# Attention and two gated layers on one core: SP's transfers of groups 1 to 7 in program order, stores an iteration behind their data, a third place for words

## The chip, the cores and the metric

The kernel runs on one core of a Trainium2 chip. What counts is the device time of one execution in microseconds. TensorE (PE) multiplies, VectorE (DVE), ScalarE (ACT) and GpSimd (POOL) work on tiles, and SyncE (SP) issues nearly all transfers (DMA).

## The reference

Three stages, all in fp32, over 4608 tokens (8 batches of 576) of 512 features:

```python
q_s = softmax(q, axis=-1)          # over the 64 features of a head, 8 heads
k_s = softmax(k, axis=2)           # over the 576 tokens
kv = einsum('bhsd,bhse->bhde', k_s, v)
x = einsum('bhsd,bhde->bhse', q_s, kv)      # then (tokens, 512)
xn = x / sqrt(mean(x * x) + 1e-6) * rms_g
x2 = (silu(xn @ w_gate) * (xn @ w_val)) @ w_out        # 512 -> 1536 -> 512
h = maximum(maximum(x2 @ w1, x2 @ w2), x2 @ w3)        # 512 -> 768
out = h @ w_out2                                       # 768 -> 512
```

## The kernel before

**Tiling.** The tokens are cut into nine groups g of 512: the first 512 of each batch, and the eight rests of 64 as group 8. An fp32 product is made of three products of split operands (high x high, low x high, high x low, the parts in fp32r). For each group the first layer runs in 12 iterations f, one for each 128 of the 1536 features: `pg`, the gate's product (12 matmuls of 128x512, `product_in`, L558 to L560), `pv`, the value's product (12 more), then t = tanh on ACT (L889), t on DVE (L890), h on DVE (L899), and h's store to DRAM by SP (L900).

**Attention in between.** Within the iterations of a group the next groups' attention is made, head pair p after head pair. For each (g, p) there are loads of kT, q, k, v and qT (q by feature); the maximum of k (`km`, L399), its broadcast through PE (`pb`, L406), the subtraction (L407), the exponential (ACT, L408) and kv (`pk`, L417); the maximum and the reciprocal sum of q, which go to DRAM (`put_stat`) and come back broadcast over the partitions (`spread_stats`, L335, four DMAs), q's softmax on POOL and ACT (`q_softmax`, L348 to L350), and x (`make_x`). When all four pairs are there, the sum of squares (`sacc`, L476) goes through PE (L509), three Newton steps on DVE give 1/rms (`z`, L517), which is stored and read back broadcast (`zb`, L524); `normalise` multiplies x by it (L540), `split_x` makes the high and low parts of x (L99, L100) that the next group's products read. For groups 0, 1 and 2, z is spread by transposes on PE instead (`spread_rstd`, L531). `turn_of` says at which pair of iterations a pair's `make_kv` is due.

**Weights ahead.** The output weights of the first layer and all of the second layer's arrive as 64-bit words. From group 1 on the class `Ahead` (`advance`, once an iteration) loads words (`st`, L216), joins them to fp32 (L225, L226), makes sums of their quarters (L238 to L241), splits seven quarters for each unit (ACT L249, POOL L250) and stores them in DRAM (L251). After group 8 the rest of the kernel, products with seven quarters of each matrix in place of eight, reads h and these quarters back and fills TensorE.

**What sets the order.** The kernel is written as one sequential program. The Tile framework's scheduler lists each engine's instructions by priority and its own estimates of time; `tc.issue_after(ins)` adds an edge that orders an instruction behind another. SP takes its list in order, so a DMA that waits (for a tile, or for a store that it reads) holds all behind it. Buffers are tiles with a tag; a tile waits for the readers of the one that had its place before.

## Time and the profile before

| | us |
|---|---|
| median of 3 runs | 1550.04 |
| lowest, highest | 1545.99, 1551.12 |
| the profiled execution | 1553.54 |
| its span | 1551.4 |
| TensorE busy in it | 1494.7 (96%) |
| VectorE, ScalarE, GpSimd busy | 1057.0, 608.0, 447.4 |

The mean granted clock of TensorE is 0.987. The profiled execution stands 3.5 us above the median of the runs, so what is read in the trace belongs to a time of 1553.54. Busy shares are averages over stages: the iterations of groups 1 to 8 and the part after group 8 are read apart.

### The profile page before, as it was taken

The page shows a single profiled execution, that of the slowest core. Times are in us where ns is not written, and L with a number is a line of the kernel's source. Part 1 is how long each engine was busy: PE and PEld are TensorE (multiplying, and loading weights), DVE is VectorE, ACT ScalarE, POOL GpSimd, SP SyncE. Part 2 cuts the span into 40 slices and gives each one's busy share as a digit, 9 for nine tenths or more (in the row PEclk, how much of TensorE's full clock was granted, in tenths as well). Part 3 has the DMA queues.
Part 4 walks back from the last instruction along what each step waited for, and adds up shares of the span by engine and source line. Part 5 has one row for each costly group of instructions (what it writes and reads, how often), then busy time and mean ns, then how long its engine had stood idle before and what let it go on. Part 6 is the DMA issues. An engine that isn't in the chain of part 4 may idle for free.

```text
span 1551.4 us, 19834 instructions
## 1 busy us (share of the span) xinstructions
PE 1494.7 (96%) x6692; PEld 1229.2 (79%) x6692; DVE 1057.0 (68%) x1777; ACT 608.0 (39%) x1197; POOL 447.4 (29%) x379
## 2 busy tenths in 40 slices
PE   5899999899999999999999999999999999999999
PEld 4677778787878788887877888888888888888887
DVE  6997575666675766364679889927938938837722
ACT  7764333333434343342445445512413413413311
POOL 0012424242524343434347657201111111101100
PEclk9999999999999999999999999999999999999999
DMA  8866777767776766677773453346486486485573
GB/s 274 293 208 183 221 205 239 213 214 221 225 219 214 219 211 198 211 260 278 281 236 130 149 193 116 126 162 238 149 309 225 159 312 223 156 310 189 174 267 108
DMA packets 159333, 330.30 MB, mean 213 GB/s; under 512 B 31104, under 2 KB 55680, under 8 KB 159232
## 3 DMA queue, kind: packets, MB, share of 16 engines
q1 hardware_dynamic: 155776, 322.74, 63.7%
q10 hardware_dynamic: 3456, 6.29, 1.1%
q8 instruction: 53, 0.87, 0.2%
q14 instruction: 48, 0.39, 0.1%
HBM read 246.42 MB, written 82.55 MB: 212 GB/s over the span
## 4 chain that ended last, share of the span: by engine, by line
PE 46%; DVE 5%; DMA 2%; issue 2%; POOL 1%; ACT 0%; SPq 0%; DVEq 0%; ACTq 0%; POOLq 0%
PE p_a L566 4%; PE p_a L565 4%; PE p_a L564 4%; PE o_acc L565 3%; PE o_acc L566 3%; PE o_acc L564 3%; PE p_G L564 2%; PE p_G L566 2%; PE p_G L565 2%; PE o_a L564 2%; PE o_a L566 2%; PE o_a L565 2%; DMA w_dram<-wq 1%; PE p_V L566 1%; PE p_V L565 1%
## 5 line engine op out<-in xcount | busy, mean ns | idle before, releaser
L988 POOL TENSOR_TENSOR temps_wl<-temps_wl,temps_wh 128x512 f32<-128x512 f32 x36 | 48.2, 1339 | 348.5 <-ACT temps_wh L987 273.8
L250 POOL TENSOR_TENSOR wq<-st,wq 128x256 fp32r<-128x256 f32 x126 | 104.0, 841 | 126.9 <-ACT wq L249 111.1
L890 DVE SCALAR_TENSOR_TENSOR t<-t,pg 128x512 f32<-128x512 f32 x106 | 72.5, 684 | 75.6 <-ACT t L889 74.9
L899 DVE SCALAR_TENSOR_TENSOR h<-t,pv 128x512 f32<-128x512 f32 x108 | 73.6, 681 | 29.6 <-PE pv L560 25.4
L249 ACT CAST wq<-st 128x256 fp32r<-128x256 f32 x126 | 51.4, 423 | 93.3 <-DMA w_dram<-wq 49.6
L385 POOL TENSOR_TENSOR q<-q,qm 128x512 f32<-128x512 f32 x28 | 31.4, 1123 | 186.9 <-PE pk L417 95.0
L348 POOL TENSOR_TENSOR qT<-qT,stat 128x512 f32<-128x512 f32 x28 | 38.8, 1386 | 144.0 <-DMA stat<-stats 43.9
L979 DVE TENSOR_TENSOR temps_wl<-temps_wl,p_a 128x512 f32<-128x512 f32 x72 | 49.2, 683 | 37.3 <-POOL temps_wl L988 37.1
L889 ACT ACTIVATE t<-pg 128x512 f32<-128x512 f32 x106 | 62.5, 590 | 24.8 <-PE pg L560 22.2
L225 DVE TENSOR_SCALAR st<-st 128x512 int32<-128x512 int32 x36 | 19.3, 537 | 68.5 <-DMA st<-in_w_out 42.4
L417 PE MATMUL pk<-v,k 128*128 128x129 f32 x300 | 43.5, 294 | 21.6 <-ACT k L408 18.5
L983 ACT COPY temps_wh<-p_G 128x512 f32<-128x512 f32 x36 | 21.1, 587 | 105.7 <-PE p_G L566 105.5
L564 PE MATMUL p_a<-x_wh,chunk 128*128 128x512 f32 x160 | 62.2, 389 | 0.0
L565 PE MATMUL p_a<-x_wh,chunk 128*128 128x512 f32 x160 | 62.2, 389 | 0.0
L566 PE MATMUL p_a<-x_wh,chunk 128*128 128x512 f32 x160 | 62.2, 389 | 0.0
L564 PE MATMUL p_a<-x_wl,chunk 128*128 128x512 f32 x160 | 62.2, 389 | 0.0
L565 PE MATMUL p_a<-x_wl,chunk 128*128 128x512 f32 x160 | 62.2, 389 | 0.0
L566 PE MATMUL p_a<-x_wl,chunk 128*128 128x512 f32 x160 | 62.2, 389 | 0.0
L417 PEld LDWEIGHTS pk<-v,k 128*128 128x128 f32 x300 | 40.0, 204 | 28.0 <-ACT k L408 23.4
L349 ACT ACTIVATE qT<-qT 128x512 f32<-128x512 f32 x28 | 17.7, 632 | 101.5 <-POOL qT L348 101.5
L985 DVE TENSOR_TENSOR temps_wl<-temps_wh,p_V 128x512 f32<-128x512 f32 x36 | 24.6, 684 | 43.9 <-PE p_V L566 43.9
L715 POOL TENSOR_TENSOR h_X<-h_Y,h_X 128x512 f32<-128x512 f32 x24 | 42.6, 1783 | 28.7 <-DVE o_xl L100 15.9
(1202 smaller groups left out, 4885.1 us busy)
## 6 DMA issues: line engine op xcount, KB each, us to landing
chunk<-w_dram SPq DMA_DIRECT2D x112, 768.0 KB, 4.4
w_dram<-wq SPq DMA_DIRECT2D x126, 256.0 KB, 3.5
h_dram<-h SPq DMA_DIRECT2D x108, 256.0 KB, 3.4
stat<-stats SPq DMA_DIRECT2D x112, 128.0 KB, 3.3
words<-in_w SPq DMA_DIRECT2D x24, 512.0 KB, 6.7
chunk<-w_dram SPq DMA_DIRECT2D x48, 256.0 KB, 3.7
k<-in_k SPq DMA_DIRECT2D x30, 320.0 KB, 4.3
v<-in_v SPq DMA_DIRECT2D x30, 320.0 KB, 4.9
```

The lines of the kernel that those rows point to most:

```text
L249: nc.scalar.copy(t[:, 0, :], src)
L250: nc.gpsimd.tensor_sub(t[:, 1, :], src, t[:, 0, :].bitcast(F32))
L417: nc.tensor.matmul(pk[:, 0 : P + 1], k_t[g, p][:, c, :], v_t[g, p][:, c, :], start=(c == 0), stop=(c == 4))
L564: nc.tensor.matmul(pt, ah, bh, start=first, stop=False, skip_group_check=onto)
L565: nc.tensor.matmul(pt, ah, bl, start=False, stop=False, skip_group_check=onto)
L566: nc.tensor.matmul(pt, al, bh, start=False, stop=last, skip_group_check=onto)
L715: nc.gpsimd.tensor_sub(x, y, x)
L889: nc.scalar.activation(t, pg, AF.Tanh, scale=0.5)
L890: nc.vector.scalar_tensor_tensor(t, t, 1.0, pg, op0=ALU.add, op1=ALU.mult)
L899: lows.append(nc.vector.scalar_tensor_tensor(h, t, 0.5, pv, op0=ALU.mult, op1=ALU.mult))
L979: nc.vector.tensor_add(y, x, pt)
L988: nc.gpsimd.tensor_add(w, u2, s5)
```

## The change

Five things are changed. (1) `sp` issues SP's DMAs; from group 1 to the start of group 8 each is ordered behind the one before it in the program. (2) Stores of h, kv, quarters and 1/rms go into a list `later`, which the head of the next iteration issues. (3) Three tiles (`rooms`, in the tags o5, o6, o7) are made once: their plane 0 holds zb, t of odd iterations and qT of odd pairs, the other planes hold four places for split quarters and a third place for words. `advance` loads words at its start, into a place that was released at least one call before. (4) The loads of a pair are in two halves (kT at an even iteration, k and v at the odd one); the statistics of q go to DRAM at the next iteration's start and are read back one iteration later; q's softmax and product come an iteration later; zb is read at the head of iteration at + 2, where `at` is 7 (9 for group 2). (5) In group 8 the load of h's last quarter (W) moves from f = 0 to f = 11.

```diff
+
+        if queue["kept"] and queue["last"] is not None:
+            with tc.issue_after(queue["last"]):
+                ins = nc.sync.dma_start(dst, src).ins
+        else:
+            ins = nc.sync.dma_start(dst, src).ins
+        queue["last"] = ins
+
+    later, rooms = [], {}
+
     class Weights:
 
 
...
+        def release(self, i):
+            if self.held[i] is None or not self.last:
+                self.free.append((self.held[i], self.now + 1))
 
         def load(self):
             i = self.loaded
-            if i < len(self.sources):
-                t = two.tile([P, 2 * N], I32, tag="st", name=f"st2_{i}")
-                nc.sync.dma_start(t, self.sources[i].bitcast(I32))
+            if i < len(self.sources) and self.free and self.free[0][1] <= self.now:
+                t = self.free.pop(0)[0]
+                self.held.append(t)
+                if t is None:
+                    t = two.tile([P, 2 * N], I32, tag="st", name=f"st2_{i}")
+                sp(t, self.sources[i].bitcast(I32))
                 words = t.rearrange("p (n t) -> p n t", t=2)
                 self.st.append((words[:, :, 0], words[:, :, 1]))
...
+            elif self.spots:
+                t = self.spots.pop(0)
+                self.spots.append(t)
+                t = t.rearrange("p (i n) -> p i n", i=2).bitcast(F32R)
             else:
                 t = two.tile([P, 2, N // 2], F32R, tag="y", name=name, bufs=3)
             nc.scalar.copy(t[:, 0, :], src)
             nc.gpsimd.tensor_sub(t[:, 1, :], src, t[:, 0, :].bitcast(F32))
-            nc.sync.dma_start(dst, t.bitcast(F32))
+            if self.spots:
+                later.append((dst, t.bitcast(F32)))
+            else:
+                sp(dst, t.bitcast(F32))
...
+            self.last = last
+            self.load()
             self.apart = f is None
...
+    def load_first(g, p):
         if g < NB:
             kT_t[g, p] = pair_tile(one, [P, 576], F32, "kT", g, p)
-            nc.sync.dma_start(kT_t[g, p], kt[g, p])
+            sp(kT_t[g, p], kt[g, p])
...
+
+    def load_second(g, p):
         if g < NB:
             k_t[g, p] = pair_tile(two, [P, 5, P], F32, "k", g, p)
-            nc.sync.dma_start(k_t[g, p], k[g, p])
+            sp(k_t[g, p], k[g, p])
...
+        qT[g, p] = rooms["qT"] if p % 2 else two.tile([P, N], F32, tag="qT", name=f"qT_{g}_{p}", bufs=1)
+        sp(qT[g, p], qt[g - BY_FEATURE, p])
...
-        put_stat(g, p, 1, qr)
+        qrec[g, p] = qr
...
-        put_stat(g, p, 0, qm)
+        qmax[g, p] = qm
...
-        nc.sync.dma_start(kv_dram[p, :, g, :], raw)
+        if g == 0:
+            sp(kv_dram[p, :, g, :], raw)
+        else:
+            later.append((kv_dram[p, :, g, :], raw))
...
-            nc.sync.dma_start(rstd_dram[g].rearrange("(r t) -> r t", t=4), z)
-            zb = wpool.tile([P, N], F32, tag="o5", name=f"zb_{g}")
-            nc.sync.dma_start(zb, rstd_dram[g].unsqueeze(0).to_broadcast([P, N]))
-            rstd[g] = None, zb
+            later.append((rstd_dram[g].rearrange("(r t) -> r t", t=4), z))
+
+    def read_rstd(g):
+        sp(rooms["zb"], rstd_dram[g].unsqueeze(0).to_broadcast([P, N]))
+        rstd[g] = None, rooms["zb"]
...
+        if g == 1 and f == 0:
+            queue["kept"] = True
+            planes = [wpool.tile([P, 3, N], F32, tag=tag, name=f"rooms_{tag}") for tag in ("o5", "o6", "o7")]
+            rooms.update({name: x[:, 0, :] for name, x in zip(("zb", "t", "qT"), planes)})
+            second.spots = [x[:, i, :] for i in (1, 2) for x in planes[0:2]]
+            second.free.append((planes[2][:, 1:3, :].rearrange("p i n -> p (i n)").bitcast(I32), 0))
+        if nxt is None and f == 0:
+            queue["kept"] = False
+            second.spots = []
+        for dst, src in later:
+            sp(dst, src)
+        later.clear()
...
@@ -838,30 +890,37 @@
             for t in due(-1):
                 make_x(*t)
             for t in due(0):
-                q_by_feature(*t)
+                q_softmax(*t)
                 make_kv(*t)
+            for t in due(1):
+                put_stat(*t, 1, qrec[t])
+                load_by_feature(*t)
+            if due(2):
+                for t in due(2):
+                    load_first(*t)
+                with tc.issue_after(lows[-1].ins):
+                    for t in due(2):
+                        first_stats(*t)
+        else:
             for t in due(2):
-                load_pair(*t)
+                put_stat(*t, 0, qmax[t])
+                load_second(*t)
             for t in due(1):
-                load_by_feature(*t)
                 spread[t] = spread_stats(*t)
             if due(2):
                 with tc.issue_after(lows[-1].ins):
                     for t in due(2):
-                        first_stats(*t)
-        else:
-            if due(2):
-                with tc.issue_after(lows[-1].ins):
-                    for t in due(2):
                         k_max(*t)
-            for t in due(2):
-                q_stats(*t)
+                        q_stats(*t)
             for t in due(1):
                 k_exp(*t)
-                q_softmax(*t)
+            for t in due(0):
+                q_by_feature(*t)
         if nxt is not None and nxt >= BY_FEATURE:
             if f == at:
                 token_rstd(nxt)
+            if f == at + 2 and nxt not in COMPACT:
+                read_rstd(nxt)
             if f == 10:
...
-            t = wpool.tile([P, N], F32, tag="o6", name=f"t_{g}_{f}")
...
-        nc.sync.dma_start(h_dram[g][f // 3][:, f % 3, :], h)
+        later.append((h_dram[g][f // 3][:, f % 3, :], h))
...
                 second.load()
+                second.load()
             second.advance(f, nxt is None)
         if nxt is None:
...
-                for name in "XZYW":
+                for name in "XZY":
                     load_h(0, name)
+            if f == NF1 - 1:
+                load_h(0, "W")
...
+    for dst, src in later:
+        sp(dst, src)
```

DVE in group 2 before, round iteration 8, where group 3's x (xraw_3_p) is multiplied by zb_3 and the maximum is taken from k of group 4's pair 0 (k_4_0):

```order
L540 TENSOR_TENSOR xraw_3_0_2255<-xraw_3_0_2255,zb_3_2720 128x512
L890 SCALAR_TENSOR_TENSOR t_2_8_2789<-t_2_8_2789,pg_2_8_2776 128x512
L341 TENSOR_SCALAR qs_4_1_2818<-qs_4_1_2818 128x8
L540 TENSOR_TENSOR xraw_3_1_2399<-xraw_3_1_2399,zb_3_2720 128x512
L343 RECIPROCAL qr_4_1_2821<-qs_4_1_2818 128x8
L540 TENSOR_TENSOR xraw_3_2_2518<-xraw_3_2_2518,zb_3_2720 128x512
L899 SCALAR_TENSOR_TENSOR h_2_8_2805<-t_2_8_2789,pv_2_8_2792 128x512
L399 TENSOR_REDUCE km_4_1_2816<-kT_4_1_2757 128x1
L407 TENSOR_TENSOR k_4_0_2647<-k_4_0_2647,pb_4_0_2824 128x640
```

The same place now; the line of dots leaves out the nine rows up to t_2_10:

```order
L949 SCALAR_TENSOR_TENSOR t_2_8_2744<-t_2_8_2744,pg_2_8_2731 128x512
L958 SCALAR_TENSOR_TENSOR h_2_8_2760<-t_2_8_2744,pv_2_8_2747 128x512
L435 TENSOR_REDUCE km_4_1_2779<-kT_4_1_2723 128x1
L376 TENSOR_REDUCE qs_4_1_2781<-q_4_1_2613 128x8
L443 TENSOR_TENSOR k_4_0_2656<-k_4_0_2656,pb_4_0_2786 128x640
...
L949 SCALAR_TENSOR_TENSOR t_2_10_2877<-t_2_10_2877,pg_2_10_2864 128x512
L580 TENSOR_TENSOR xraw_3_0_2233<-xraw_3_0_2233,rooms_o5_1432 128x512
L580 TENSOR_TENSOR xraw_3_1_2373<-xraw_3_1_2373,rooms_o5_1432 128x512
L580 TENSOR_TENSOR xraw_3_2_2490<-xraw_3_2_2490,rooms_o5_1432 128x512
L580 TENSOR_TENSOR xraw_3_3_2606<-xraw_3_3_2606,rooms_o5_1432 128x512
L958 SCALAR_TENSOR_TENSOR h_2_10_2893<-t_2_10_2877,pv_2_10_2880 128x512
```

k_4_0's subtraction has moved ahead of group 3's four products with zb, which now stand two iterations later, behind t_2_10.

SP in group 2 before, round iterations 10 and 11, with the broadcast (stat_4_2) of the statistics of group 4's pair 2, the words st2_9 and k's load:

```order
L328 DMA stats_4_2_173<-qr_4_2_2958 128x2x4
L251 DMA w1_dram_7_149<-wq_3_2_3095 128x512
L335 DMA stat_4_2_3047<-stats_4_2_173 64x512
L900 DMA h_dram_2_3_117<-h_2_10_2950 128x512
L292 DMA kT_4_3_3040<-in_kt 128x576
L335 DMA stat_4_2_3047<-stats_4_2_173 64x512 x3
L251 DMA w1_dram_10_152<-wq_3_1_3099 128x512
L216 DMA st2_9_3103<-in_w1_out 128x1024
L900 DMA h_dram_2_3_117<-h_2_11_3008 128x512
L297 DMA k_4_3_3042<-in_k 128x640
```

SP in group 2 now, round iterations 9 and 10 (rooms_o5 in the second row is zb, in the later ones places of split quarters; rooms_o7 is qT):

```order
L142 DMA stat_4_0_2774<-stats_4_0_171 64x512 x4
L142 DMA rooms_o5_1432<-rstd_3_194 128x512
L142 DMA h_dram_2_3_117<-h_2_9_2819 128x512
L142 DMA w1_dram_4_146<-rooms_o5_1432 128x512
L142 DMA w1_dram_16_158<-rooms_o6_1433 128x512
L142 DMA w1_dram_13_155<-rooms_o5_1432 128x512
L142 DMA stats_4_1_172<-qr_4_1_2784 128x2x4
L142 DMA rooms_o7_1434<-in_qt 128x512
L142 DMA kT_4_2_2852<-in_kt 128x576
L142 DMA q_4_3_2854<-in_q 128x512
L142 DMA st2_9_2895<-in_w1_out 128x1024
L142 DMA kv_dram_200<-kv_raw0_213 128x128
L142 DMA h_dram_2_3_117<-h_2_10_2893 128x512
```

The broadcasts stand together, behind the loads of k and v and ahead of the zb read; h_2_9's store follows at the head of iteration 10, with the statistics, and the words st2_9 stand with the loads.

POOL in group 1 before, near the end, with the last sum of squares of group 2 (sacc_2) and q of group 3:

```order
L476 TENSOR_TENSOR sacc_2_1569<-sacc_2_1569,sq_2_2_1843 128x512
L348 TENSOR_TENSOR qT_3_0_1971<-qT_3_0_1971,stat_3_0_1973 128x512
L350 TENSOR_TENSOR qT_3_0_1971<-qT_3_0_1971,stat_3_0_1973 128x512
L385 TENSOR_TENSOR q_3_1_1872<-q_3_1_1872,qm_3_1_1980 128x512
L476 TENSOR_TENSOR sacc_2_1569<-sacc_2_1569,sq_2_3_1963 128x512
```

POOL at the same place now:

```order
L421 TENSOR_TENSOR q_3_1_1854<-q_3_1_1854,qm_3_1_1963 128x512
L515 TENSOR_TENSOR sacc_2_1567<-sacc_2_1567,sq_2_3_1953 128x512
L275 TENSOR_TENSOR rooms_o6_1433<-st2_3_1812,rooms_o6_1433 128x256
L421 TENSOR_TENSOR q_3_2_1961<-q_3_2_1961,qm_3_2_2116 128x512
L384 TENSOR_TENSOR qT_3_0_1957<-qT_3_0_1957,stat_3_0_2010 128x512
L386 TENSOR_TENSOR qT_3_0_1957<-qT_3_0_1957,stat_3_0_2010 128x512
```

qT_3_0's two steps, which read the broadcast statistic, have moved from ahead of the last sum to behind it.

## Rows read from the trace of the kernel before

**Rows 1.** Windows (busy us of PE, PEld, DVE, ACT, POOL; clock, DMA share, GB/s).

```profile
611.60:684.30 72.70, 72.70 (x346) 61.32 (x346) 37.51 (x71) 29.45 (x59) 25.32 (x29) 1.00 0.67 213
756.50:1551.40 794.90, 787.17 (x3457) 647.44 (x3455) 558.59 (x766) 283.07 (x489) 200.01 (x127) 1.00 0.57 197
125.80:756.50 630.70, 605.67 (x2765) 502.78 (x2764) 389.34 (x762) 237.51 (x466) 239.31 (x229) 0.98 0.74 226
```

**Rows 2.** TensorE's waits: us in total, times, longest.

```profile
PE pk L417 <- ACT k L408: 18.5, 12, 4.2
...
PE pv L558 <- DVE h L899: 3.6, 1, 3.6
PE pv L509 <- POOL sacc L476: 3.2, 1, 3.2
PE rstd L531 <- DVE z L517: 2.8, 1, 2.8
```

**Rows 3.** Windows as in group 1, the six at the low clock.

```profile
121.30:124.70 3.40, 3.40 (x10) 2.55 (x10) 3.40 (x7) 3.18 (x6) 0.00 (x0) 0.50 0.63 169
186.20:193.00 6.80, 6.80 (x21) 5.64 (x22) 6.26 (x17) 2.95 (x7) 4.13 (x6) 0.50 0.69 211
278.30:285.10 6.80, 5.09 (x17) 4.50 (x18) 6.80 (x14) 2.47 (x5) 2.14 (x2) 0.50 0.80 241
363.70:367.10 3.40, 3.40 (x10) 2.62 (x9) 3.35 (x10) 0.63 (x1) 1.51 (x1) 0.50 1.00 269
442.20:449.00 6.80, 6.15 (x19) 5.32 (x20) 6.80 (x11) 2.22 (x4) 2.60 (x2) 0.50 0.78 236
711.90:718.60 6.70, 6.02 (x14) 4.82 (x15) 2.00 (x4) 1.80 (x5) 1.74 (x3) 0.50 0.75 237
```

**Rows 4.** Timeline, groups 2 and 5: start, duration, engine, [idle before, releaser].

```profile
268.33 0.32 SPq L524 DMA_DIRECT2D zb<-rstd  x1
...
274.56 0.69 DVE L540 TENSOR_TENSOR xraw<-xraw,zb 128x512 f32<-128x512 f32 x1 [2.28 <-DMA zb<-rstd]
...
278.38 0.81 DVE L407 TENSOR_TENSOR k<-k,pb 128x640 f32<-128x640 f32 x1
...
279.22 0.74 ACT L408 ACTIVATE k<-k 128x640 f32<-128x640 f32 x1 [0.81 <-DVE k L407]
...
280.01 2.52 PE L417 MATMUL pk<-v,k 128*128 128x129 f32 x10 [4.17 <-ACT k L408]
...
522.09 0.38 PE L417 MATMUL pk<-v,k 128*128 128x129 f32 x1 [1.05 <-ACT k L408]
```

**Rows 5.** Timeline, group 3: words, their join, pk.

```profile
295.86 0.43 SPq L216 DMA_DIRECT2D st<-in_w_out  x1
...
302.75 0.43 DVE L225 TENSOR_SCALAR st<-st 128x512 int32<-128x512 int32 x1 [3.31 <-DMA st<-in_w_out]
...
309.17 0.60 PE L417 MATMUL pk<-v,k 128*128 128x129 f32 x3 [0.74 <-ACT k L408]
```

**Rows 6.** SP's waits (total, times, longest), and zb's landing.

```profile
SPq L335 <- DMA stats<-qm: 18.4, 9, 3.6
SPq L335 <- DMA stats<-qr: 18.0, 16, 2.8
...
DMA to landing us min/median/max: 4.6/5.2/7.0
```

**Rows 7.** Timeline, group 1: POOL round the last sum of squares.

```profile
178.90 1.29 POOL L348 TENSOR_TENSOR qT<-qT,stat 128x512 f32<-128x512 f32 x1 [8.73 <-DMA stat<-stats]
...
184.69 1.27 POOL L476 TENSOR_TENSOR sacc<-sacc,sq 128x512 f32<-128x512 f32 x1
```

**Rows 8.** Timeline, group 8: words and their join.

```profile
696.02 0.44 SPq L216 DMA_DIRECT2D st<-in_w_out  x1
...
704.08 1.01 DVE L225 TENSOR_SCALAR st<-st 128x512 int32<-128x512 int32 x1 [3.04 <-DMA st<-in_w_out]
```

**Rows 9.** Timeline, group 0: words in DVE's chain.

```profile
119.81 0.41 DVE L225 TENSOR_SCALAR st<-st 128x512 int32<-128x512 int32 x1
```

More of the change, by code (lines that the diff above doesn't have):

```diff
@@ L134, in attention_moe_moe, with sp @@
     wh, wl = {}, {}
+    queue = {"last": None, "kept": False}
+    def sp(dst, src):
+        if queue["kept"] and queue["last"] is not None:
[5 more added lines that the diff above has]
+    later, rooms = [], {}
     class Weights:
@@ L150, in load @@
                     src = w1[f].rearrange("p j n -> p (j n)")[:, h * HALF : (h + 1) * HALF]
-                    nc.sync.dma_start(t, src.bitcast(I32))
+                    sp(t, src.bitcast(I32))
                     words = t.rearrange("p (n t) -> p n t", t=2)
@@ L204, in __init__ @@
             self.loaded, self.st, self.now, self.apart = 0, [], 0, False
-            self.issued, self.turn = [], False
+            self.issued, self.turn, self.spots = [], False, []
+            self.free, self.held, self.last = [(None, 0), (None, 0)], [], False
             self.steps = []
@@ L208, in __init__ @@
                 self.steps += [(self.join, (2 * u,)), (self.join, (2 * u + 1,)), (self.sums, (u,))]
-                self.steps += [(self.quarter, (u, n)) for n in (A11, A12, S3, S4)] + [(self.load, ())]
-                self.steps += [(self.quarter, (u, n)) for n in (A22, S1, S2)] + [(self.load, ())]
+                self.steps += [(self.quarter, (u, n)) for n in (A11, A12, S3, S4)] + [(self.release, (2 * u,))]
+                self.steps += [(self.quarter, (u, n)) for n in (A22, S1, S2)] + [(self.release, (2 * u + 1,))]
+        def release(self, i):
+            if self.held[i] is None or not self.last:
+                self.free.append((self.held[i], self.now + 1))
         def load(self):
             i = self.loaded
-            if i < len(self.sources):
-                t = two.tile([P, 2 * N], I32, tag="st", name=f"st2_{i}")
-                nc.sync.dma_start(t, self.sources[i].bitcast(I32))
+            if i < len(self.sources) and self.free and self.free[0][1] <= self.now:
[4 more added lines that the diff above has]
+                sp(t, self.sources[i].bitcast(I32))
                 words = t.rearrange("p (n t) -> p n t", t=2)
@@ L271, in advance @@
                 writes = step == self.quarter
-                cost = 0 if step == self.load else 1 if writes else 2
+                cost = 0 if step == self.release else 1 if writes else 2
                 if cost > room or writes and not last and f > 9:
@@ L286, in load_q @@
         q_t[g, p] = pair_tile(two, [P, 8, 64], F32, "q", g, p)
-        nc.sync.dma_start(q_t[g, p], q[g, p])
+        sp(q_t[g, p], q[g, p])
     def load_pair(g, p):
+        load_first(g, p)
+        load_second(g, p)
+    def load_first(g, p):
         if g < NB:
             kT_t[g, p] = pair_tile(one, [P, 576], F32, "kT", g, p)
-            nc.sync.dma_start(kT_t[g, p], kt[g, p])
+            sp(kT_t[g, p], kt[g, p])
         if g < BY_FEATURE:
             load_q(g, p)
+    def load_second(g, p):
         if g < NB:
             k_t[g, p] = pair_tile(two, [P, 5, P], F32, "k", g, p)
-            nc.sync.dma_start(k_t[g, p], k[g, p])
+            sp(k_t[g, p], k[g, p])
             if (g, p, "v") in early or len(v_rooms) < 2:
@@ L308, in load_pair @@
             v_t[g, p] = place
-            nc.sync.dma_start(place[:, :, 0:P], v[g, p])
+            sp(place[:, :, 0:P], v[g, p])
         else:
@@ L313, in load_pair @@
                 t = two.tile([P, 4, P], F32, tag=("k", "v")[i], name=f"kv8_{p}_{i}")
-                nc.sync.dma_start(t, kv_dram[p, :, 4 * i : 4 * i + 4, :])
+                sp(t, kv_dram[p, :, 4 * i : 4 * i + 4, :])
                 kv8[p].append(t)
     qsum = {}
-    qT, spread = {}, {}
+    qT, spread, qmax, qrec = {}, {}, {}, {}
     def load_by_feature(g, p):
-        qT[g, p] = two.tile([P, N], F32, tag="qT", name=f"qT_{g}_{p}", bufs=1)
-        nc.sync.dma_start(qT[g, p], qt[g - BY_FEATURE, p])
+        qT[g, p] = rooms["qT"] if p % 2 else two.tile([P, N], F32, tag="qT", name=f"qT_{g}_{p}", bufs=1)
+        sp(qT[g, p], qt[g - BY_FEATURE, p])
     def put_stat(g, p, i, stat):
         dst = stats_dram[NPAIR * g + p][i].rearrange("a (r t) -> r a t", t=4)
-        nc.sync.dma_start(dst, stat.rearrange("r (a t) -> r a t", a=2))
+        sp(dst, stat.rearrange("r (a t) -> r a t", a=2))
     def spread_stats(g, p):
@@ L534, in spread_rstd @@
         else:
-            zb = wpool.tile([P, N], F32, tag="o5", name=f"zb_{g}")
+            zb = rooms["zb"]
         nc.scalar.copy(zb, pr)
@@ L572, in attention_moe_moe @@
         load_pair(0, p)
-    nc.sync.dma_start(gain, rms_g)
+    sp(gain, rms_g)
     first.load(0)
@@ L671, in out_weights @@
                 t = wpool.tile([P, 2, 2, N // 2], F32R, tag=tag, name=f"w1q_{tag}")
-                nc.sync.dma_start(t.bitcast(F32), w1_dram[len(wq1)])
+                sp(t.bitcast(F32), w1_dram[len(wq1)])
                 wq1.append(t)
@@ L680, in load_h @@
             t = wpool.tile([P, 3, N], F32, tag=tag, name=f"h_{pr}_{name}{j}")
-            nc.sync.dma_start(t, h_dram[g][2 * half + j])
+            sp(t, h_dram[g][2 * half + j])
             for i in range(3):
@@ L881, in iteration @@
         if odd and 0 < g < NB:
-            t = wpool.tile([P, N], F32, tag="o6", name=f"t_{g}_{f}")
+            t = rooms["t"]
         else:
```

2 lines of the change are left out of this document (1 added, 1 removed).

## The prediction

> **What bounds the kernel now.** I read the sums by stage first, then the waits of TensorE, then the stretches at the low clock, and last the timeline round each wait. After group 8 (from 756.50 us) TensorE is busy 787.17 of 794.90 us with 3457 matmuls, 0.2277 us each, at clock 1.00. The eight groups ahead of it, 125.80 to 756.50, where nearly all that the change moves stands, hold 605.67 busy in 630.70 [rows 1]. So TensorE is the bound and only what makes it idle or slow can be won. An iteration's 24 matmuls take 24 x 0.2277 = 5.46 us. Group 7 shows what a group without any such loss looks like: busy for all of its 72.70 us, clock 1.00 [rows 1].
>
> Who makes TensorE wait: ACT's exponential of k (12 waits, 18.5 us), and once each DVE's h (3.6), POOL's sum of squares (3.2) and DVE's z (2.8) [rows 2]. Six stretches at a granted clock of 0.50, the lower of its two levels (1.2 against 2.4 GHz), follow or overlap such waits: TensorE was busy 3.40 + 6.80 + 5.09 + 3.40 + 6.15 + 6.02 = 30.86 us in them, half of which, 15.4, is lost [rows 3]. The waits named in this paragraph that were followed by the low clock are of 2.8 to 4.2 us; that of 1.05 at 522.09 was not [rows 2 to 4]. The waits sum to 18.5 + 3.6 + 3.2 + 2.8 = 28.1; with the clock 43.5 us are at stake.
>
> **A: the wait at iteration 9 of groups 2 to 5.** The read of 1/rms (zb) was issued at 268.33; DVE stood 2.28 us for it and multiplied at 274.56; the subtraction of k's maximum, behind three of these products, came at 278.38, the exponential at 279.22, pk at 280.01 after an idle 4.17. In four groups this idle time is 4.17, 3.50, 2.96 and 1.05 (the first and the last of them are shown) = 11.7; three of the four have a low stretch, busy 5.09 + 3.40 + 6.15 = 14.64, so 7.3 lost [rows 3, 4]. After the change DVE's rows have k_4_0's subtraction four rows behind t_2_8, and the four products eleven and more rows later, behind t_2_10. DVE was idle from 272.28; subtraction 0.81 and exponential 0.74 from there end before 274, and pk was free to start at 280.01 - 4.17 = 275.84. Nearly 2 us are in hand. Removed: 19.0, all of it.
>
> **What A puts in its place.** The products now stand two iterations behind the statistic, near the next group's start. SP's rows have the zb read behind four broadcasts at the head of iteration 9. At 0.32 to 0.43 us an issue [rows 4, 5] it leaves at about 275.4 in the time of before, and it lands 4.6, 5.2 or 7.0 us later (least, median, most) [rows 6]: at 282.4 at the latest, where t_2_10 would be done at about 281.2 (275.84, 1.3 for pk, which is half of the 2.52 that its row shows at the low clock, 2.7 for 12 matmuls, 1.3 for tanh and t). From there DVE has four products at 0.69 [rows 4], three steps of t and h, q's low part and four low parts of x, twelve of 128x512 at 0.69, k_4_1's subtraction (0.81) and two small ones (0.3): 9.4 us, so the last low part is there at 290.6. pk (1.3), two iterations (10.92) and some 2.3 of products and transposes of the attention between them bring TensorE to group 3 at about 290.3, and it wants the low parts one after another until about 292. The chain just fits. Price below: nothing; above: a wait as long as the worst landing brings it, 2.8 idle and 1.7 of clock at each of six group starts. I take 0.7 at each, 4.2, since the estimate leaves about 1 us and the single terms were seen to vary by more.
>
> **B: group 2's sum of squares.** POOL waited 8.73 us for the broadcast statistic and took q of pair 0 ahead of the last sum, which ended at 185.96, when TensorE had been idle 3.2 [rows 2, 7]. In the new rows of POOL the sum stands ahead of that q, behind an instruction of pair 1 that needs no broadcast. Idle 3.2 and half of 6.80 at the low clock, together 6.6, go.
>
> **C: the other waits for k's exponential**, 18.5 - 11.7 = 6.8 us in eight places. One of them: weight words for the joins were issued at 295.86, DVE stood 3.31 for them until 302.75, and pk waited 0.74 at 309.17 [rows 5]. With a third place the words leave an iteration or two earlier; by SP's rows st2_9 stands at about 280 where it is wanted at about 292. Where words were late this goes; where DVE and ACT have other work ahead of k it stays. Bounds 0 and 6.8 left; I leave half, 3.4.
>
> **D: group 8.** The words issued at 696.02 reached DVE at 704.08 (3.04 idle); that instruction took 1.01 where its twin at 302.75 took 0.43 [rows 5, 8]. h_8_3 was late and TensorE idle 3.6, then 6.02 at half speed: 6.6 in all [rows 2, 3]. The change takes the load of h's last quarter out of iteration 0 and so the queue at the words' place is shorter, but POOL and DVE keep their work. Bounds 0 and 6.6; half left, 3.3. The load, now at iteration 11, lands under the products of the part after, where TensorE is full; if that cover were gone it would cost its landing, some 5 us, once.
>
> **E: group 1's rstd.** Work on weight words stood inside DVE's chain (0.41 at 119.81), TensorE idle 2.8, then 3.40 at half speed: 4.5 [rows 2, 3, 9]. These words now stand behind the chain, but the transposes are asked for 10 matmuls (2.3 us) earlier. Bounds 0 and 4.5; I leave 1.0, since the h and the maximum that stood in the chain are behind it too.
>
> **Edits costed at nothing.** The stores that go an iteration later (h, kv, quarters) have their readers two groups or more later. q's softmax and product one iteration later: px that uses them moves with them, and q has the same number of iterations to the next step. The splits' room in other tiles takes away a wait for a buffer and adds none that stands on TensorE's path. If a store's delay held a tile, DVE's h would wait for SP: the cover is the second h tile, which leaves 5.46 us.
>
> SP's own queue is the disputed cost. It has some 80 issues in a group (counted in its order), near 35 of 73 us at 0.44 each [rows 1, 8], so half of its time is free. In the order of before, SP waited for the statistics' own stores ahead of the broadcasts, 18.4 us in 9 places and 18.0 in 16, 2.0 and 1.1 us each [rows 6]. The new order has nine other DMAs, 9 x 0.43 = 3.9 us, between the second statistic's store and its broadcasts, so by these rows the stand is gone. The Trainium skill, "DMA: Bandwidth & Descriptors", section "Two DMAs through the same engine are not ordered", says that placing a store and its read on one queue does not order them: the issuing engine must wait for the store's completion before it issues the read. The trace agrees that SP stands there; by that rule, in an order that nothing may overtake, everything behind the read stands too, and the sum stays as it is only as long as other issues fill the time. Without the page, the same mechanism is the fourth rival below.
>
> **The sum.** 43.5 - 3.4 (C) - 3.3 (D) - 1.0 (E) - 4.2 (new waits) = 31.6. The profiled execution took 1553.54 us (span 1551.4): 1521.9. It stood 3.5 over the median of the runs, 1550.04, so **1519 us** there.
>
> **The rivals.**
> - Forecast, 1519 (own range 1510 to 1528): 0.68.
> - x late at the starts of groups 3 to 8: if zb lands after 282.4 or DVE runs 2 us behind, 2.8 idle and 1.7 clock at six places, 27 in place of 4.2: 1541. For it: the chain just fits. Against: the worst landing seen [rows 6] still fits. 0.12.
> - pk's waits stay, since DVE's and ACT's own queues set them: only B, E and half of D are won, 6.6 + 3.5 + 3.3, less some 1.5: 1538. Against: DVE stood idle 2.28 for a DMA [rows 4]. 0.10.
> - Slower: SP stands in an order that nothing may overtake. A store of h that waits for DVE, or a broadcast that waits for a store, now holds the loads of k, v and the words behind it; before, the schedule let others pass. SP's free half of a pair of iterations is 5 to 6 us; past that, with the two iterations that loads have in hand, from 8 to 10 us a pair of iterations, each us more stands on TensorE in some 24 pairs. At 2 us more: 48 less the gain of 31.6, about 1566. Against: the free half, and the words ahead of need. 0.05.
> - The order moves but the waits only change places: 1550. 0.05.
>
> Changes under 0.3% (4.65 us) can't be told from none here. Faster by more: 0.68 + 0.12 + 0.10 less a little of these tails, 0.87. Within it 0.06, slower 0.07. The range goes from all 43.5 won (1510.0, less 3.5: 1507) to past the two middle rivals (1542).
>
> **What would show it.** Right: no row of pk waiting for ACT over 2 us in groups 2 to 5; POOL's last sum of group 2 ahead of its q; groups 2 to 6 near 73 to 76 us; fewer than three low stretches; DVE not idle for zb. Wrong: TensorE idle at the first product of a group for a low part of x; SP's waits longer for the stores of h; DVE idle for words as before; the part from group 8's end on other than 795 us.

## The result and the profile after

The changed kernel takes 1528.19 us (median of 4 runs, 1525.93 to 1528.61), beside 1548.01 for the kernel before (4 runs, 1543.64 to 1551.12): ratio 0.9871, 95% interval 0.9842 to 0.9900. The profiled execution took 1527.82 us, its span 1526.0, mean clock 0.996. It answers the 1553.54 of before: 25.7 us less, where the medians differ by 19.8, so a size read by comparing the two traces is in part the spread of single executions.

By windows (columns as in [rows 1]), groups 1 to 8 of the changed kernel and the part after group 8:

```profile
125.00:728.07 603.07, 594.25 (x2765) 494.08 (x2764) 387.65 (x764) 240.33 (x466) 234.38 (x225) 1.00 0.79 237
728.07:1526.00 797.93, 788.33 (x3457) 647.13 (x3455) 563.29 (x767) 283.14 (x491) 206.09 (x133) 1.00 0.57 198
```

The groups took 27.6 us less than in [rows 1], the part after them 3.0 more. TensorE's waits in the changed kernel (total, times, longest):

```profile
PE rstd L571 <- DVE z L556: 5.2, 2, 2.7
...
PE px L497 <- DVE ql L100: 4.0, 7, 0.9
...
PE pk L453 <- ACT k L444: 1.3, 2, 0.9
...
PE pv L548 <- POOL sacc L515: 1.0, 1, 1.0
```

Against [rows 2] the wait for k's exponential is down from 18.5 to 1.3, that for the sum of squares from 3.2 to 1.0, that for h in group 8 is gone. New are a second wait for z and seven small ones for q's low part. Of the low clock's six stretches [rows 3] two are left, of 3.41 us each: one answers to the first of before, the other stands behind the new wait for z (columns as in [rows 1]):

```profile
118.04:121.45 3.41, 3.41 (x10) 2.63 (x9) 3.25 (x6) 2.35 (x4) 0.00 (x0) 0.50 0.20 77
193.14:196.55 3.41, 3.41 (x15) 3.21 (x14) 2.95 (x5) 1.75 (x3) 2.71 (x2) 0.50 0.88 319
```

The timeline of group 2 in the changed kernel, as [rows 4]:

```profile
267.36 0.81 DVE L443 TENSOR_TENSOR k<-k,pb 128x640 f32<-128x640 f32 x1
...
270.45 0.41 SPq L142 DMA_DIRECT2D rooms_o<-rstd  x1
...
276.44 2.60 DVE L580 TENSOR_TENSOR xraw<-xraw,rooms_o 128x512 f32<-128x512 f32 x4
```

k's subtraction is 3 us ahead of the read of 1/rms (here rooms_o), and no product of this group waits for that. The group began at 208.7, so the read goes out 61.8 us into it; in the kernel before it went out after 56.8 (268.33 - 211.5). The read has become later, not earlier.

### The profile page after: what moved, and what is told of

It reads as the page before. It is cut to its first block, busy times and chain, and to the rows that moved or that the text cites. A ratio compares the mean times of both kernels' runs of the same rounds, so it can differ in the third digit from the quotient of the medians.

```text
span 1526.0 us, 19735 instructions
## 1 busy us (share of the span) xinstructions
PE 1484.5 (97%) x6692; PEld 1220.3 (80%) x6692; DVE 1060.2 (69%) x1777; ACT 609.0 (40%) x1197; POOL 447.6 (29%) x379
## 5 line engine op out<-in xcount | busy, mean ns | idle before, releaser
L949 DVE SCALAR_TENSOR_TENSOR t<-t,pg 128x512 f32<-128x512 f32 x64 | 43.8, 684 | 62.4 <-ACT t L948 61.8
L275 POOL TENSOR_TENSOR rooms_o<-st,rooms_o 128x256 fp32r<-128x256 f32 x63 | 50.4, 807 | 113.8 <-ACT rooms_o L274 109.2
L958 DVE SCALAR_TENSOR_TENSOR h<-t,pv 128x512 f32<-128x512 f32 x66 | 45.0, 682 | 24.7 <-PE pv L600 22.3
L948 ACT ACTIVATE t<-pg 128x512 f32<-128x512 f32 x64 | 37.8, 590 | 39.4 <-PE pg L600 38.8
L949 DVE SCALAR_TENSOR_TENSOR rooms_o<-rooms_o,pg 128x512 f32<-128x512 f32 x42 | 28.5, 678 | 28.8 <-ACT rooms_o L948 28.8
L757 POOL TENSOR_TENSOR h_Y<-h_W,h_Y 128x512 f32<-128x512 f32 x24 | 39.0, 1639 | 25.3 <-DMA h_W<-h_dram 24.9
L759 POOL TENSOR_TENSOR h_Z<-h_Z,h_X 128x512 f32<-128x512 f32 x24 | 40.0, 1685 | 11.0 <-DVE h_X L752 8.4
L948 ACT ACTIVATE rooms_o<-pg 128x512 f32<-128x512 f32 x42 | 24.8, 590 | 42.5 <-PE pg L600 42.4
```

The costliest lines, as they stand in the source:

```text
L275: nc.gpsimd.tensor_sub(t[:, 1, :], src, t[:, 0, :].bitcast(F32))
L759: nc.gpsimd.tensor_sub(z, z, x)
L948: nc.scalar.activation(t, pg, AF.Tanh, scale=0.5)
L949: nc.vector.scalar_tensor_tensor(t, t, 1.0, pg, op0=ALU.add, op1=ALU.mult)
L958: lows.append(nc.vector.scalar_tensor_tensor(h, t, 0.5, pv, op0=ALU.mult, op1=ALU.mult))
```

## The experiments

All times are medians; ratios are to the kernel before, which ran beside each.

**1. SP's order left to the scheduler.** In the changed kernel one line is left out, so that nothing orders SP's transfers:

```diff
-            queue["kept"] = True
```

> The changed kernel, but the order of SP's transfers in groups 1 to 7 is left to the scheduler, which then puts the first product with zb ahead of h_2_8 and of k_4_0's subtraction again in group 2, and the four products right behind the subtraction in group 3. Theory (DVE's place for these products is what costs, and SP's fixed order is what moves it): pk waits for ACT again in group 2, 2 to 4 us and the low clock behind it, less in groups 3 to 5; in all 5 to 15 us over the changed kernel, 1533 to 1543. Rival (the places, the third words and the later stores bring the gain, SP's order nothing): within 4 us of the changed kernel's 1528.

Measured 1557.88 us, ratio 1.0048 (1.0030 to 1.0066): slower than before, and far over the theory's figure. All the rest of the change without the fixed order is worth less than nothing. In group 2 a product does stand ahead of k's subtraction again and pk waits 2.27 there, as the theory has it, but that is one wait of many. TensorE's waits in this kernel:

```profile
PE pk L453 <- ACT k L444: 16.7, 8, 5.2
PE pv L548 <- POOL sacc L515: 7.1, 4, 2.7
```

and SP's own:

```profile
SPq L144 <- DMA stats<-qm: 35.2, 19, 4.2
SPq L144 <- DMA stats<-qr: 30.7, 15, 3.8
```

SP stands 65.9 us for the statistics' stores. In the kernel before it was 36.4 [rows 6], in the changed kernel 10.1, by its one row:

```profile
SPq L142 <- DMA stats<-qr: 10.1, 5, 2.9
```

In group 2 the scheduler's list has three other transfers between the second statistic's store and its first read, the changed kernel's eight. The store and the read without the fixed order, then with it:

```profile
267.86 0.37 SPq L144 DMA_DIRECT2D stats<-qr  x1
...
270.89 0.45 SPq L144 DMA_DIRECT2D stat<-stats  x1
```

```profile
260.51 0.43 SPq L142 DMA_DIRECT2D stats<-qr  x1
...
267.68 2.55 SPq L142 DMA_DIRECT2D stat<-stats  x4
```

How much of TensorE's loss comes of this stand was not tried by itself.

**2. The products' place alone.** The kernel before with an edge that keeps the four products with zb behind h of iteration 9:

```diff
-            if f == 10:
+            if f == 10 and nxt in COMPACT:
                 for p in range(4):
                     normalise(nxt, p)
+            if f == 10 and nxt not in COMPACT:
+                with tc.issue_after(lows[-1].ins):
+                    for p in range(4):
+                        normalise(nxt, p)
```

(COMPACT are groups 0 to 2, whose z is spread by transposes.)

> The kernel before with one edge more: the four products with zb in groups 2 to 7 are ordered behind the h of iteration 9, so that k's subtraction stands ahead of them; SP's order, stores and places are as before. Theory (the place of the products alone makes the waits at iteration 9): the four waits of 11.7 us and the low clock of 7.3 go, 12 to 19 us off the kernel before, so 1529 to 1536. Rival (SP's late transfers hold DVE there whatever its order): waits of over 2 us at the same place stay, and the time is within 5 us of the kernel before.

Measured 1545.94 us, ratio 0.9976 (0.9960 to 0.9992): 2.8 us off, far from the theory's 12 to 19 and in the rival's time. The rival's waits came only in part: of the four waits at iteration 9 two are gone, the others are 2.10 and 0.54, so 2.6 of 11.7 us is left there. Group 2, where the longer one is:

```profile
266.62 0.44 SPq L524 DMA_DIRECT2D zb<-rstd  x1
...
273.97 0.81 DVE L407 TENSOR_TENSOR k<-k,pb 128x640 f32<-128x640 f32 x1
...
276.67 2.15 PE L417 MATMUL pk<-v,k 128*128 128x129 f32 x10 [2.10 <-ACT k L408]
```

The group began at 210.3, so the read, 56.3 into it, is as late as before (56.8): at iteration 9 the products' place alone does most of the work. But pk waits 15.1 us in all, still 12 times. The timeline at the end of group 3 in this kernel:

```profile
367.73 0.68 DVE L100 TENSOR_TENSOR xl<-xraw,xh 128x512 fp32r<-128x512 f32 x1
...
370.26 0.81 DVE L407 TENSOR_TENSOR k<-k,pb 128x640 f32<-128x640 f32 x1
...
371.10 0.74 ACT L408 ACTIVATE k<-k 128x640 f32<-128x640 f32 x1 [3.57 <-DVE k L407]
...
371.89 1.39 PE L417 MATMUL pk<-v,k 128*128 128x129 f32 x8 [2.49 <-ACT k L408]
```

DVE now makes two of x's low parts just ahead of the next pair's k, and pk waits there, at iteration 11 (2.49, 2.39 and 2.50 at the ends of groups 3, 4 and 5). Most of the wait moved by two iterations.

**3. The order alone.** The kernel before with SP's transfers of groups 1 to 7 chained in its own program order, nothing else:

```diff
-        nc.sync.dma_start(h_dram[g][f // 3][:, f % 3, :], h)
+        sp(h_dram[g][f // 3][:, f % 3, :], h)
...
+        if g == 1 and f == 0:
+            queue["kept"] = True
+        if nxt is None and f == 0:
+            queue["kept"] = False
```

(`sp` is the function of the change; all of SP's transfers of these groups go through it, of which one is shown.)

> The kernel before with SP's transfers of groups 1 to 7 chained in its own program order and nothing else: 1/rms is read back right behind its store, statistics right behind theirs, stores stand where their data are made. Theory (a fixed order pays only when the program is laid out for it): SP stands in it for DVE's chain and for landings, the loads behind come late, and pk, the sums of squares and the words wait more; 5 to 40 us over the kernel before, 1555 to 1590. Rival (program order in itself is what brings the gain): 5 to 20 us under it, 1530 to 1545.

Measured 1534.57 us, ratio 0.9892 (0.9862 to 0.9922). My theory falls, the rival holds: the order alone brings 15 of the 20 us. The theory took the statistics' reads to stand right behind their stores in this order; in the trace seven other transfers lie between (store at 252.53, first read at 264.00), and SP stands 9.7 us for the second statistic's store. Its timeline in group 2:

```profile
258.80 0.32 SPq L142 DMA_DIRECT2D rstd<-z  x1
...
260.88 0.32 SPq L142 DMA_DIRECT2D zb<-rstd  x1
...
265.31 1.29 DVE L551 TENSOR_TENSOR xraw<-xraw,zb 128x512 f32<-128x512 f32 x2 [1.74 <-DMA zb<-rstd]
...
267.78 0.81 DVE L418 TENSOR_TENSOR k<-k,pb 128x640 f32<-128x640 f32 x1
```

DVE takes two of the products ahead of k's subtraction as the scheduler has it, and TensorE does not wait in iteration 9 of any group. The group began at 206.6, so k's subtraction stands 61.2 us into it; in the kernel before 278.38 - 211.5 = 66.9. The read was issued 54.3 into the group against 56.8, and DVE's first product came 4.4 us behind it against 6.2 [rows 4]. Of the 5.7 us 4.3 are the earlier first product, 1.4 the fewer steps of DVE between it and the subtraction.

So with two products still ahead of the subtraction, an earlier read and DVE's shorter way behind it clear iteration 9. The changed kernel clears it the other way: its read is later than before, and the subtraction stands ahead of the products. Neither the products' place nor the late read is the cause by itself: the place alone takes 9.0 of the 11.7 us (experiment 2), the order alone all of it.

The order brings more than this one wait: that for the sum of squares falls from 3.2 to 1.1, that for h in group 8 is gone, and DVE stands 30.9 us for weight words where it stood 64.4. Groups 1 to 8 take 610.7 us (630.7 before), the part after them 799.0 (794.9). How the 15 us split among these was not tried. What is left over the changed kernel is mostly pk's waits at iteration 1 (1.5 to 2.0 in each of groups 2 to 6):

```profile
PE pk L428 <- ACT k L419: 12.1, 8, 2.4
```

**4. Stores at once.** The changed kernel, `later` not used:

```diff
-        later.append((h_dram[g][f // 3][:, f % 3, :], h))
+        sp(h_dram[g][f // 3][:, f % 3, :], h)
```

(and the same for kv, quarters and 1/rms.)

> The changed kernel, SP's fixed order kept, but every store (h, kv, quarters, 1/rms) is issued where its data are made instead of at the head of the next iteration. Theory (in a fixed order a store that waits for its data holds the loads behind it, so the later list is what makes the order bearable): SP stands for DVE's h and POOL's quarters in the middle of an iteration, and loads and broadcasts come later; 4 to 15 us over the changed kernel, 1532 to 1543. Rival (SP has half of its time free, so the place of the stores does not matter): within 2 us of 1528.

Measured 1535.57 us, ratio 0.9910 (0.9889 to 0.9932): inside the theory's range. px waits for q's low part 7.0 us in place of 4.0, o_acc once 4.1. The loss is shown; that it comes of SP's stand for h and the quarters is the theory's reading.

**5. Two places for words.** The changed kernel without the third place:

```diff
-            second.free.append((planes[2][:, 1:3, :].rearrange("p i n -> p (i n)").bitcast(I32), 0))
...
-                second.load()
```

(the last line is the first load into that place.)

> The changed kernel without the third place for words. Theory (the third place brings the words ahead of need, which took away the small waits of pk and the wait for h in group 8): waits for k's exponential come back in part, and more words are left for the part after group 8; 3 to 8 us over the changed kernel, 1531 to 1536. Rival (DVE's order alone took these waits away): within 2 us of 1528.

Measured 1552.10 us, ratio 1.0019 (1.0003 to 1.0034): 24 us lost, three times the theory's upper figure. Little of it lies where the theory put it. The windows of this kernel, and two waits in the part after group 8:

```profile
127.80:734.07 606.27, 595.10 (x2765) 493.93 (x2764) 375.47 (x758) 236.82 (x461) 222.33 (x220) 1.00 0.77 231
734.07:1552.80 818.73, 793.32 (x3456) 650.71 (x3455) 562.65 (x774) 285.90 (x496) 203.78 (x137) 0.99 0.56 196
```

```profile
786.42 0.48 SPq L144 DMA_DIRECT2D st<-in_w_out  x1
...
789.47 0.42 ACT L274 CAST wq<-st 128x256 fp32r<-128x256 f32 x1 [5.27 <-DMA w_dram<-wq]
...
792.68 0.68 ACT L245 ACTIVATE st<-st 128x512 f32<-128x512 f32 x1 [0.71 <-DMA st<-in_w_out]
...
793.24 2.18 ACT L99 CAST o_xh<-h_X 128x512 fp32r<-128x512 f32 x4
...
795.58 0.77 PE L604 MATMUL o_acc<-o_qh,w1q_wl 128*128 128x512 f32 x1 [7.44 <-ACT o_xh L99]
...
823.54 0.42 ACT L274 CAST wq<-st 128x256 fp32r<-128x256 f32 x1 [2.64 <-DMA w_dram<-wq]
...
824.49 0.79 PE L604 MATMUL o_acc<-o_qh,w1q_wh 128*128 128x512 f32 x1 [8.75 <-ACT temps_wh L801]
```

The groups take 3.2 us more than with three places, the part after them 20.8. There 16 quarters are left (13 in the changed kernel), the last 90 us behind group 8's end. Ahead of the work of ACT that the products want stand its steps on quarters and words, and these wait: 5.27 and 2.64 us for an earlier quarter's store, 0.71 for late words. The two waits of TensorE, 7.44 and 8.75, are 16.2 of the 20.8 us.

**6. Two places, refilled at once.** As 5, but a released place is loaded again in the same call:

```diff
-                self.free.append((self.held[i], self.now + 1))
+                self.free.append((self.held[i], self.now))
+                self.load()
```

> The changed kernel with two places for words, each filled again at once when it is released, in place of an iteration later. Theory (the kernel with two places lost 24 us because a place stays empty for an iteration, so that 16 quarters were left after group 8, the last of them 90 us behind its end; the third place pays for that delay): some 10 quarters are left, the last within 50 us of the end, and the part after group 8 is 795 to 799 us; 1528 to 1535. Rival (three words in flight are needed in themselves): 1540 or more, with the waits of 7 and 9 us in the part after group 8.

Measured 1529.66 us, ratio 0.9872 (0.9842 to 0.9901): as fast as the changed kernel. 9 quarters are left, the last at 48 us, as the theory has it; the part after group 8 took 799.96, just over its 799, in the profiled execution, which is the slowest of the six runs. In this kernel the third place only pays for the iteration that a place stays empty.

**7. h's last quarter at iteration 0 of group 8.**

```diff
-                for name in "XZY":
+                for name in "XZYW":
...
-            if f == NF1 - 1:
-                load_h(0, "W")
```

> The changed kernel with the load of h's last quarter back at iteration 0 of group 8. Theory (the 3.0 us that the part after group 8 grew by are that load's, since GpSimd stands 24.9 us in all for it and its sums and DVE's low parts come late): the part after group 8 is 795 us again and group 8 stays without a wait, 2 to 3 us off the changed kernel, about 1525.5. Rival (they are of the weight words, of which more are split after group 8): the part stays at 798 and the time within 1 us of 1528. Second rival (the load at iteration 0 delays the words again, as before): a wait for h in group 8 of 2 to 4 us and the low clock, 1531 to 1535.

Measured 1527.98 us, ratio 0.9859 (0.9837 to 0.9880): no difference from the changed kernel. The part after group 8 takes 797.47, as the first rival has it, and group 8 has no wait: the load's place costs and brings nothing here.

**8. Quarters in the last iterations of groups 6 and 7.**

```diff
-        def advance(self, f, last):
+        def advance(self, f, last, free=False):
...
-                if cost > room or writes and not last and f > 9:
+                if cost > room or writes and not last and not free and f > 9:
...
-            second.advance(f, nxt is None)
+            second.advance(f, nxt is None, g >= 6)
```

> The changed kernel, but in groups 6 and 7 quarters of weights may be split in iterations 10 and 11 too. Theory (the part after group 8 is longer by 3.0 us because 13 quarters in place of 9 are left for it): about 6 quarters fewer are left, the waits of its first 60 us shrink, and the part is 795 to 796 us; 2 to 3 us off the changed kernel, 1525 to 1526. Rival (the part's length comes from h's last quarter or from the state of DVE there, not from the words): fewer quarters left and yet 798 us.

Measured 1527.26 us (1520.81 to 1534.81), ratio 0.9862 (0.9834 to 0.9890). The part after group 8 is shorter still than the theory's 795 to 796, with 6 quarters left (13 in the changed kernel), but group 7 pays for it, 76.10 us in place of 72.70:

```profile
730.53:1523.90 793.37, 786.53 (x3456) 647.54 (x3455) 557.09 (x764) 280.31 (x483) 205.58 (x127) 1.00 0.57 197
```

```profile
601.71 0.32 PE L492 MATMUL px<-qh,kv 128*128 128x64 f32 x1 [1.55 <-ACT qh L391]
```

**9. Group 2's transposes of 1/rms at iteration 10.**

```diff
-        if nxt in COMPACT and f == (10 if nxt < BY_FEATURE else at):
+        if nxt in COMPACT and f == 10:
```

(its products at iteration 11.)

> The changed kernel with group 2's transposes of 1/rms at iteration 10 instead of 9, and its four products at iteration 11. Theory (the new wait of 2.75 us there, and 3.41 us at the low clock behind it, are of a chain on DVE that starts late because the maximum of k ahead of it waits for its load): the wait goes and none takes its place, 3 to 4.5 us off the changed kernel, 1524 to 1525. Rival (x of group 2 is then late at the group's start): a wait of 1 to 4 us at its first products instead, 1528 or more.

Measured 1526.11 us, ratio 0.9851 (0.9833 to 0.9869). The wait of 2.75 is gone and group 2 starts without one. It is 2 us off in place of the theory's 3 to 4.5, which the intervals don't part from the changed kernel.

**10 to 12. Put together.** Experiment 10 has edits 8 and 9 and orders q's sum behind q's low part; 11 is the same with quarters in the last iterations of group 7 alone (`g >= 7`); 12 is the same as 10 without edit 8. The new edit:

```diff
+            made = [q_by_feature(*t) for t in due(0)]
...
+                with tc.issue_after(made[-1].ins if made and made[-1] is not None else lows[-1].ins):
+                    for t in due(2):
+                        q_stats(*t)
...
-            for t in due(0):
-                q_by_feature(*t)
```

> The changed kernel with group 2's transposes later, quarters in iterations 10 and 11 of groups 6 and 7, and q's sum behind q's low part, so that the first product of x finds this earlier. If the three losses are separate they add: 4.4 for the transposes, 2 to 3 for the quarters, 1 to 3 for the low part, 1518 to 1521. Rival (one wait hides another, or DVE's other work is late instead): 1524 or more.

> As the kernel with all three edits, but quarters go into iterations 10 and 11 of group 7 alone. Theory (the wait of 1.87 us for q's copy at the start of group 7, and the low clock of 6.83 us behind it, come of the quarters that group 6's last iterations took on): group 7 is 72.7 us again, 5 us off that kernel, 1519 to 1522. Rival (the wait comes of q's sum being later): it stays, 1525.

> The changed kernel with group 2's transposes later and q's sum behind q's low part, without the quarters. If the edits act apart: no wait of px for ql over 0.5 us in groups 3 to 6, none at group 7's start, the part after group 8 at 798 us; 1521 to 1524. If q's sum behind the low part is what makes group 7 wait: 1526 or more.

Measured 1525.73, 1526.27 and 1525.52 us, ratios 0.9846 (0.9828 to 0.9864), 0.9842 (0.9815 to 0.9868) and 0.9831 (0.9804 to 0.9859). All three miss their theory's time. In the first px no longer waits for the low part, but group 7 takes 78.10 us: its rival, that the gains do not add, holds. In the second group 7 is back at 72.70 as the theory says, but pk waits 1.0, 0.8 and 1.4 in groups 3 to 5 instead and the part after group 8 is 798.65. The third has the best profile (span 1521.0) and the best ratio. None is shown to beat the changed kernel.

## Why the prediction was right, and where not

The direction was right and 1528.19 lies in the range, just past the edge of the forecast's own (1510 to 1528). The waits that it named as removable are the ones that went. What it did not see is where the gain comes from: it took SP's fixed order for a cost in dispute and booked the gains to DVE's order, the places and the loads. Alone that order brings 15 of the 20 us, and without it the rest loses 9 (experiments 3 and 1). In the profiled execution the sum said 1521.9 and 1527.82 came:

- **A, pk at iteration 9: 19.0 to go.** All went but 0.9 (at 423.62), and in the changed kernel by the step that the prediction named: k's subtraction stands ahead of the products and of the read. That this step wins the 19.0 by itself is wrong: alone it took 9.0 of the 11.7 idle there, but 2.8 us of the time, and made new waits (experiment 2). Nor is it the only way: the order alone cleared the place too (experiment 3).
- **What A puts in its place: 4.2 at x's low parts.** No such wait came; px waits for q's low part instead, 4.0 in seven places, a wait that the prediction did not name. The size is right by chance.
- **B: 6.6 to go.** 1.0 idle is left. The order alone leaves 1.1, so POOL's new place is not the only way here either.
- **C and D: half left, 3.4 and 3.3.** Of pk's other waits 0.3 is left, of group 8's nothing: 6.4 better than the sum. D's reason was wrong: with the load of h's last quarter back at iteration 0 group 8 has no wait either (experiment 7), and the order alone removes it (experiment 3).
- **E: 1.0 left.** 2.5 idle and half of 3.41 are left, 4.2. The term was mis-sized by 3.2. With the words out of it, DVE's chain from the variance to z takes 7.0 us (110.17 to 117.17) where it took 9.3 (110.96 to 120.29). But TensorE asks for z 2.9 us earlier, at 117.32 - 2.49 = 114.83 against 120.44 - 2.76 = 117.68. The changed kernel, then the one before:

```profile
117.32 0.62 PE L571 MATMUL rstd<-ident,z 128*128 128x128 f32 x4 [2.49 <-DVE z L556]
```

```profile
120.44 0.62 PE L531 MATMUL rstd<-ident,z 128*128 128x128 f32 x4 [2.76 <-DVE z L517]
```

  The prediction named the earlier asking and left too little for it. Much of the 7.0 us are three steps stretched beside GpSimd (last section); such steps stood in the chain before, too.
- **Not seen: group 2's z.** 2.75 idle and 1.7 of clock. At 187.38 DVE takes km after 2.68 us of idle for kT's load, and the chain is queued behind:

```profile
180.34 0.33 SPq L142 DMA_DIRECT2D h_dram<-h  x1
...
181.75 0.43 SPq L142 DMA_DIRECT2D kT<-in_kt  x1
...
187.38 0.75 DVE L435 TENSOR_REDUCE km<-kT 128x1 f32<-128x576 f32 x1 [2.68 <-DMA kT<-in_kt]
...
192.71 0.69 PE L571 MATMUL rstd<-ident,z 128*128 128x128 f32 x4 [2.75 <-DVE z L556]
```

  kT's load was issued behind a store of h that SP had stood for until DVE's h was done (at 180.34). It is the rival "slower" in small: DVE now stands for kT in 8 places, 11.7 us (one, 2.3 us, before), and at one of them TensorE stands too. An earlier load was not tried.
- **Costed at nothing, the part after group 8: 3.0.** Not h's last quarter (experiment 7). With 6 quarters left in place of 13 the part took 793.4 (experiment 8) and 794.9 (experiment 10), so the words may have to do with it; but with 8 to 10 left it took 796 to 800 in five kernels, and 794.9 before with 9, so the count alone does not set it. What does stays open.

These make 0.9 + 1.0 - 6.4 + 3.2 - 0.2 + 4.4 + 3.0 = 5.9, the difference. That the sum came so near is in part luck: misses of 12.5 on one side and 6.6 on the other. The rest of the error is the step from the profiled execution to the median. I took off the 3.5 by which the former stood over the latter before (which gives 1518.4, put down as 1519), but the changed kernel's profiled execution stands 0.4 under its median. In the 23 runs of the kernel before beside the first experiments (1544.16 to 1557.03, median 1548.75) 1553.54 is one of the slower executions; a difference of one execution was taken for a constant.

Of the signs of being wrong two came. SP stood longer for the stores of h, 189.9 us in 71 places against 135.4 in 64, and of TensorE's waits only that for group 2's z was traced to such a stand; and the part after group 8 is not 795. Of the signs of being right, DVE's wait for zb is down from 14.7 us in 6 places to 2.4 in 2, not gone, and groups 2 to 6 take 76.2 us on average.

The rival "pk's waits stay, since DVE's and ACT's queues set them" did not come: 1.3 of 18.5 us is left. "The waits only change places" is what the products' place does alone (experiment 2). The rival "slower: SP stands in its fixed order" did not come either, and its ground fails: SP waits less for statistics in the fixed order (10.1 us, and 9.7 and 1.0 with the order alone) than in the scheduler's (36.4, and 65.9 in experiment 1). The Trainium skill, "DMA: Bandwidth & Descriptors", section "Two DMAs through the same engine are not ordered", has the issuing engine wait for a store's completion ahead of the read. The traces agree that SP stands there, and show the other half: who fixes the order also fixes how much lies between the two, three transfers or eight in experiment 1.

## What to carry to other kernels

When a queue stands for landings, look at how far each read lies behind its store in the queue's own list: an explicit order that puts other transfers between can shorten the stand, and can be worth more than the places and buffers around it. That the shorter stand is what paid here is not shown; the earlier words and the earlier read came with it. Test parts both ways, alone on the kernel before and left out of the kernel after: here the order alone gave 15 us, all the rest alone lost 9, both gave 20. A trace of the part alone also tells whether it works as in the whole: iteration 9 was cleared with an earlier read in the one and by DVE's order in the other. A delay (here the release of a place) and the buffer that pays for it belong together; left out singly, the buffer looks worth 24 us.

## What was not expected of the hardware

Small steps of DVE ended together with GpSimd's instruction beside them. In the chain for 1/rms of group 1 in the changed kernel three steps on 128x4 took 1.25, 1.00 and 1.20 us where the same lines take 0.16 some microseconds later:

```profile
111.19 1.56 POOL L384 TENSOR_TENSOR qT<-qT,stat 128x512 f32<-128x512 f32 x1 [13.29 <-DMA stat<-stats]
111.51 1.25 DVE L554 SCALAR_TENSOR_TENSOR a<-z 128x4 f32<-128x4 f32 x1
...
112.71 1.56 POOL L421 TENSOR_TENSOR q<-q,qm 128x512 f32<-128x512 f32 x1
...
113.29 1.00 DVE L555 TENSOR_TENSOR a<-a,var 128x4 f32<-128x4 f32 x1
...
114.23 1.27 POOL L386 TENSOR_TENSOR qT<-qT,stat 128x512 f32<-128x512 f32 x1
...
114.32 1.20 DVE L556 SCALAR_TENSOR_TENSOR z<-a,z 128x4 f32<-128x4 f32 x1
115.55 0.16 DVE L554 SCALAR_TENSOR_TENSOR a<-z 128x4 f32<-128x4 f32 x1
```

111.19 + 1.56 = 112.75 and 111.51 + 1.25 = 112.76; 112.71 + 1.56 = 114.27 and 113.29 + 1.00 = 114.29; 114.23 + 1.27 = 115.50 and 114.32 + 1.20 = 115.52: each ends with the GpSimd step beside it. The three add 3.0 us to the chain, more than the 2.49 that TensorE waits for it. The kernel before had such steps in the same chain, of 1.26, 1.01 and 0.49 us; the first:

```profile
111.81 1.73 POOL L348 TENSOR_TENSOR qT<-qT,stat 128x512 f32<-128x512 f32 x1 [13.33 <-DVE z L512]
```

```profile
112.29 1.26 DVE L515 SCALAR_TENSOR_TENSOR a<-z 128x4 f32<-128x4 f32 x1
```

Here too 111.81 + 1.73 = 113.54 and 112.29 + 1.26 = 113.55. The Trainium skill, "SBUF — State Buffer", section "Who interferes with whom", says that a VectorE instruction with two inputs in SBUF contends with a GpSimd instruction that reads SBUF. These rows agree; no run here took GpSimd's step away, so that the wait would go with it was not tried.
